# A planned attention-and-two-layers kernel: other transfer times in its planner, single score groups in the first batch, and sums of weights on GpSimd

## The chip, the cores and the metric

The kernel runs on one core of a Trainium2 chip. The metric is the device time of one execution in microseconds (us), the median of several runs. The engines are TensorE (PE in the rows; PEld is its loading of weights), VectorE (DVE), ScalarE (ACT), GpSimd (POOL) and SyncE (SP). SP and POOL issue the transfers. Each engine takes its instructions strictly in order, so an instruction that waits holds up all that are queued behind it on that engine.

## The reference

Four batches of attention with 12 heads, 448 positions and head width 64, and then two layers of a plain two-matrix network on the 1792 x 768 result:

```
scores = cap * tanh(q @ k.T / sqrt(64) / cap)          # cap = 30
attn   = exp(scores - max) / (sum(exp(scores - max)) + 1e-9)
x      = (attn @ v), heads joined                      # 1792 x 768
h      = max(x @ w_in, 0);  x = (h * h) @ w_out        # first layer, 768 -> 2048 -> 768
h2     = max(x @ w_in2, 0); out = (h2 * h2) @ w_out2   # second layer, same sizes
```

Everything is float32. The weights arrive as 64-bit words and are rounded on the chip to float32.

## The kernel before, in words

**Numbers.** TensorE multiplies in a reduced format; a float32 value is split into a high part (a rounded copy) and a low part (value minus copy), and a product takes three matmuls: high x high, high x low, low x high. In the first batch the attention weights times the values (L524, with `whole` set) are done in plain float32 instead, two matmuls in the trace for each in the code.

**First part** (until about 709 us). `unit(s)` is one row of weight tiles times one batch of the first layer: 34 units for each of four batches (`NU = 34`, `NS = 136` in all), L370 to L372. While batch b goes through its units, the attention of batch b + 1 is done in between; only batch 0 has its attention ahead of all units. A batch has six `pair`s of heads. A pair has four score groups a, b, c, d (`GROUPS`): for each, scores (L493), tanh (L498), exp (L503), then attention times values (L524). Afterwards the sums of exp are copied (`den`, L558, two ScalarE instructions), inverted (L561), multiplied in (L565) and split into `xb` (L570, L212). Scores live in the ring `sc`, which has two places; tanh and exp work in place, and in the first batch the place is free again when exp has been written to `pe`.

**Rounding weights.** `round_words` loads words (L256, L259), scales them on ScalarE (L265), puts the bits together on VectorE (L268, L271, L274) and stores the float32 weights to DRAM from the POOL queue (L277). For the first layer this runs inside batch 0's units. For the second layer it runs in 17 *blocks* (`round_block`) during batches 1 to 3: each block rounds two tiles into `wx` (ring `wg`, three buffers), and when both stores have landed, adds and subtracts their quarters in place in a chain of four sums (`one_sum`, L306) and stores the results (L310). When those stores land, the buffers of the block are free for the scaling of a later block, which stands in ScalarE's queue among the splits of weights that feed TensorE (`wh`, L332; then `wl`, L212 on VectorE; three buffers each).

**Second part** (from about 709 us). The second layer takes two batches at a time with seven products instead of eight, of weight tiles and of the sums of tiles (L821 to L823). Its first evacuated product goes to a tile `one` (L841) whose memory was that of `wx`; it waits until the last block's stores have landed.

**The order.** `Plan` collects all operations with an engine, a cost in ns, a place (about one per unit) and dependencies, and `emit` simulates them: on every engine it takes, out of a window of 40 by place, the operation that could start first by its own clock. The order that comes out is the program's; the chip's waits are then as the chip has them. A transfer is planned with 700 ns before it starts, its bytes by a rate (L105) and a fixed time until it has landed (L106). The planner knows the engine names "POOL" (issuing of transfers) and, in the change, "GP" as two queues with clocks of their own; on the chip they are one.

Of the kernel before, what the change touches and what calls it, by code (L numbers as in the profile page):

```python
# [25 lines left out]
NU = len(UNITS)  # L26
# [10 lines left out]
class Plan:  # L37
# [12 lines left out]
    def op(self, engine, cost, emit, place, deps=(), take=(), drop=(), after=()):  # L50


        self.ops.append([engine, cost, emit, place, list(deps), list(take), list(drop), None, list(after)])
        return len(self.ops) - 1

    def emit(self, sizes):
        rings = {n: [(0.0, i) for i in (range(k) if isinstance(k, int) else k)] for n, k in sizes.items()}
        for o in self.ops:
            o[5] = [r if isinstance(r, tuple) else (r, [None]) for r in o[5]]
            o[6] = [r if isinstance(r, tuple) else (r, [None]) for r in o[6]]  # L60
        for o in self.ops:
            o[4] = [d() if callable(d) else d for d in o[4]]
        waiting, clock = {}, {}
        for i in sorted(range(len(self.ops)), key=lambda i: (self.ops[i][3], i)):
            waiting.setdefault(self.ops[i][0], []).append(i)
            clock[self.ops[i][0]] = 0.0
        turn = {n: [] for n in rings}
        for i in sorted(range(len(self.ops)), key=lambda i: (self.ops[i][3], i)):
            for r, _ in self.ops[i][5]:
                turn[r].append(i)  # L70
        dma = 0.0
        while any(waiting.values()):
            best = None
            now = self.ops[waiting["PE"][0]][3] if waiting["PE"] else 1e9
            for e, ids in waiting.items():
                found = None
                for at, i in enumerate(ids[:self.WINDOW]):
                    _, _, _, place, deps, take, _, _, after = self.ops[i]
                    if place > now + self.AHEAD:
                        break  # L80
                    if any(self.ops[d][7] is None for d in deps + after):
                        continue
                    t = max([clock[e]] + [self.ops[d][7] + self.DELAY for d in deps])
                    names = [r for r, _ in take]
                    if any(len(rings[r]) < names.count(r) or turn[r][0] != i for r in names):
                        continue
                    for r in names:
                        t = max(t, sorted(rings[r])[names.count(r) - 1][0])
                    if found is None or t < found[0] - 1:
                        found = t, e, at  # L90
                    if t <= clock[e]:
                        break
                if found and (best is None or found[0] < best[0]):
                    best = found
            t, e, at = best
            op = self.ops[waiting[e].pop(at)]
            for r, cell in op[5]:
                got = min(rings[r], key=lambda x: x[0])
                rings[r].remove(got)
                cell[0] = got[1]  # L100
                turn[r].pop(0)
            op[2]()
            if e in ("SP", "POOL"):
                clock[e] = t + 60
                dma = max(dma, t + 700) + op[1] / 400  # L105
                op[7] = dma + 1300  # L106
            else:
                clock[e] = op[7] = t + op[1]
            for r, cell in op[6]:
                rings[r].append((op[7], cell[0]))  # L110
# [47 lines left out]
def pipeline(ctx: ExitStack, tc: tile.TileContext, qk, v, capt, rcap, eps, win, wout, w32, sums, x2, out):  # L158
# [13 lines left out]
    nc = tc.nc  # L172
# [27 lines left out]
    op = plan.op  # L200
# [4 lines left out]
    def dve(n, rate=1.04):  # L205
        return rate * n + 67
# [87 lines left out]
    def round_block(g, i, k, t0):  # L294


        c0, c1 = (0, HC) if g == 0 else FP[1][k]
        n = c1 - c0
        us = [unit_of(g, r, k) for r in (i, i + (HF if g == 0 else HC))]
        ms = [round_words(1, u, t0 + 2.5 * r, ring="wg") for r, u in enumerate(us)]  # L300

        def one_sum(q):
            a11, a12, a21, a22 = (m["f"][:, h * n:h * n + n] for m in ms for h in range(2))
            out, a, b, how = [(a22, a21, a22, ALU.add), (a21, a11, a21, ALU.subtract),
                              (a11, a22, a11, ALU.subtract), (a12, a12, a11, ALU.subtract)][q]
            nc.vector.tensor_tensor(out, a, b, op=how)  # L306

        def store():
            for r, m in enumerate(ms):
                nc.gpsimd.dma_start(sums[g, i][:, 2 * r:2 * r + 2, c0:c1], m["f"][:, :2 * n].rearrange("p (h c) m -> p h c m", h=2))  # L310

        o = [stored[1, u] for u in us]
        for q in range(4):
            o = [op("DVE", dve(n * 128), lambda q=q: one_sum(q), t0 + 5, o)]
        summed[g, i, k] = op("POOL", 4 * n * 128 * 512, store, t0 + 5, o, drop=[("wg", m["wf"]) for m in ms])

    def load_w(s):
        l, u = s // NS, s % NU
        nk = n_of(l, u)
        m = rings_of()  # L320

        def load():
            m["f"] = w_f[m["wf"][0]]
            nc.sync.dma_start(like(l, u, m["f"]), kept(l, u))

        split_w(s, m, [op("SP", nk * 128 * 512, load, s - 4, [stored[l, u]], take=[("wf", m["wf"])])], n=nk)
# [99 lines left out]
    def pair(b, j, t0, step, whole, on_act):  # L426
# [55 lines left out]
        for gi, tiles in enumerate(GROUPS):  # L482
            s, n = groups[gi], len(tiles) * S
# [41 lines left out]
                                         start=t == 0 and n == 0, stop=t == 3 and n == len(passes) - 1)  # L525

            t1 = t0 + dt[gi]
            if gi == 0:
                scored = []

                def both(scored=scored):
                    for x in scored:
                        x()

                first = op("PE", mm(6), both, t1, [parts], take=[("sc", x["at"]) for x in groups[:2]])
                scored.append(scores)
            elif gi == 1:
                scored.append(scores)
            if gi < 2:
                o = first  # L540
            else:
                o = op("PE", mm(3), scores, t1, [parts], take=[at], drop=["qkh", "qkl"] if gi == 3 else [])
# [46 lines left out]
    for u in range(NU):  # L589
        round_words(0, u, start + 9 + 4 * u if u < EARLY else u - 3.5, u if u < 3 or u >= EARLY else None)  # L590
        if 3 <= u < EARLY:
            load_w(u)
    for b in range(B):
        if b + 1 < B:
            for j in range(NP):
                pair(b + 1, j, b * NU + 0.5 + 4.9 * j, 1.25, (b + 1, j) in WHOLE, True)
        for u in range(NU):
            s = b * NU + u
            if b:
                load_w(s)  # L600
                if s % 6 == 4:
                    round_block(*blocks[(s - NU) // 6], s)
            unit(s)

    two = {}
# [453 lines left out]
```

## Time and profile before

| what | us |
|---|---|
| median of 3 runs | 1118.12 |
| the 3 runs | 1116.62, 1118.12, 1132.72 |
| the profiled execution, whole time | 1121.04 |
| its span, first to last instruction | 1119.3 |
| TensorE busy in the span | 1083.4 |
| VectorE busy | 840.2 |
| ScalarE busy | 725.7 |
| GpSimd busy | 74.3 |

The sum of the prediction is made against the profiled execution, 1121.04 us, which is 2.92 us above the median. A busy engine is one with an instruction of its own under way; a matmul's end is modelled, so busy TensorE isn't TensorE at its peak. Of a wait the profile names the instruction that came last.

### The profile page before, as it was taken

What the parts mean: (1) busy time and instruction counts of PE and PEld (TensorE: products, weight loads), DVE (VectorE), ACT (ScalarE), POOL (GpSimd) and SP (SyncE); (2) the same over time, 40 slices, a digit from 0 to 9 for tenths busy, and PEclk for the clock granted to TensorE, in tenths of its full rate; (3) what the DMA queues carried; (4) which work ended last, traced back from release to release, by engine and by line L of the source; (5) the groups of instructions that cost most, each with busy time, mean ns of one, the idle gap of its engine ahead of it and who ended that gap; (6) DMA issues with size and microseconds to landing.
All of it is one profiled execution on the core that took longest, in us unless ns stands there. A gap on an engine that the chain in (4) does not pass through costs nothing.

```text
span 1119.3 us, 14984 instructions
## 1 busy us (share of the span) xinstructions
PE 1083.4 (97%) x5320; PEld 939.8 (84%) x5320; DVE 840.2 (75%) x1092; ACT 725.7 (65%) x1053; POOL 74.3 (7%) x130
## 2 busy tenths in 40 slices
PE   5889999999999999999998999999999999999997
PEld 3457777888888888888887889899999999999997
DVE  4787889888889787888866885455897775569852
ACT  5798887867998777998645843344656534465641
POOL 0000011101001010001111111000000000000000
PEclk9999999999999999999999999999999999999999
DMA  8376787968666789575666886433346543333442
GB/s 223 91 235 224 233 251 226 283 201 295 191 176 227 203 274 287 164 213 172 190 220 222 305 261 205 130 107 105 99 129 208 167 142 104 113 99 121 130 133 71
DMA packets 82788, 207.92 MB, mean 186 GB/s; under 512 B 10768, under 2 KB 37264, under 8 KB 82704
## 3 DMA queue, kind: packets, MB, share of 16 engines
q1 hardware_dynamic: 72240, 163.61, 49.8%
q0 software_dynamic: 10464, 43.26, 10.1%
q8 instruction: 43, 0.70, 0.3%
q14 instruction: 41, 0.34, 0.1%
HBM read 158.07 MB, written 48.76 MB: 185 GB/s over the span
## 4 chain that ended last, share of the span: by engine, by line
PE 83%; issue 6%; DMA 4%; ACT 3%; DVE 3%; POOL 1%; SPq 0%; DVEq 0%; ACTq 0%; POOLq 0%
PE bank L821 12%; PE bank L822 12%; PE bank L823 12%; PE bank L370 11%; PE bank L372 11%; PE bank L371 10%; PE bank L524 9%; PE bank L493 5%; DMA wo<-wx 3%; ACT pe L503 1%; DVE wx L306 1%; ACT bank L498 1%; ACT d L558 1%; DMA wi<-wx 1%; POOL so L310 0%
## 5 line engine op out<-in xcount | busy, mean ns | idle before, releaser
L332 ACT ACTIVATE wh<-wf 128x768 fp32r<-128x768 f32 (+1 forms) x248 | 204.0, 824 | 230.6 <-PE bank L822 134.7
L212 DVE TENSOR_TENSOR wl<-wf,wh 128x768 fp32r<-128x768 f32 (+1 forms) x248 | 229.0, 925 | 143.2 <-ACT wh L332 139.5
L370 PE MATMUL bank<-xb,wh 128*128 128x448 f32 x384 | 146.7, 382 | 3.1 <-ACT wh L332 3.1
L370 PE MATMUL bank<-gh,wh 128*128 128x448 f32 x384 | 144.9, 377 | 0.0
L372 PE MATMUL bank<-gh,wl 128*128 128x448 f32 x384 | 141.0, 367 | 2.0 <-DVE wl L212 2.0
L372 PE MATMUL bank<-xb,wl 128*128 128x448 f32 x384 | 140.9, 367 | 1.8 <-DVE wl L212 1.8
L371 PE MATMUL bank<-gl,wh 128*128 128x448 f32 x384 | 140.9, 367 | 0.0
L371 PE MATMUL bank<-xb,wh 128*128 128x448 f32 x384 | 140.4, 366 | 0.3 <-DVE xb L212 0.3
L822 PE MATMUL bank<-xc,wh 128*128 128x448 f32 x384 | 140.2, 365 | 0.0
L821 PE MATMUL bank<-xc,wh 128*128 128x448 f32 x378 | 138.2, 366 | 1.2 <-ACT one L841 1.2
L823 PE MATMUL bank<-xc,wl 128*128 128x448 f32 x378 | 138.1, 365 | 0.0
L823 PE MATMUL bank<-xb,wl 128*128 128x448 f32 x294 | 107.4, 365 | 0.0
L821 PE MATMUL bank<-xb,wh 128*128 128x448 f32 x294 | 107.4, 365 | 0.0
L822 PE MATMUL bank<-xb,wh 128*128 128x448 f32 x288 | 105.2, 365 | 0.0
L498 ACT ACTIVATE bank<-bank,caps 128x896 f32<-128x896 f32 x96 | 83.2, 882 | 29.3 <-PE bank L493 28.3
L370 PEld LDWEIGHTS bank<-xb,wh 128*128 128x128 f32 x384 | 72.1, 188 | 18.4 <-issue 8.4
L561 DVE RECIPROCAL d<-d 128x448 f32<-128x448 f32 x24 | 70.8, 2949 | 20.6 <-ACT d L558 20.4
L370 PEld LDWEIGHTS bank<-gh,wh 128*128 128x128 f32 x384 | 72.5, 189 | 15.2 <-issue 9.2
L372 PEld LDWEIGHTS bank<-xb,wl 128*128 128x128 f32 x384 | 72.1, 188 | 9.6 <-DVE wl L212 3.9
L372 PEld LDWEIGHTS bank<-gh,wl 128*128 128x128 f32 x384 | 72.6, 189 | 8.3 <-DVE wl L212 2.4
L371 PEld LDWEIGHTS bank<-xb,wh 128*128 128x128 f32 x384 | 72.2, 188 | 8.0 <-issue 2.0
L371 PEld LDWEIGHTS bank<-gl,wh 128*128 128x128 f32 x384 | 72.6, 189 | 5.9 <-issue 0.6
(136 smaller groups left out, 1950.1 us busy)
## 6 DMA issues: line engine op xcount, KB each, us to landing
ww<-win_dram SPq DMA_DIRECT2D x27, 768.0 KB, 5.6
wf<-wi SPq DMA_DIRECT2D x48, 384.0 KB, 4.6
ww<-wout_dram SPq DMA_DIRECT2D x18, 768.0 KB, 6.3
wf<-wo SPq DMA_DIRECT2D x38, 320.0 KB, 4.1
raw<-qk_dram SPq DMA_DIRECT2D x48, 240.0 KB, 5.9
wf<-si SPq DMA_DIRECT2D x60, 192.0 KB, 2.5
wf<-wo SPq DMA_DIRECT2D x28, 384.0 KB, 3.9
wf<-wi SPq DMA_DIRECT2D x48, 192.0 KB, 2.5
```

The costliest lines, as they stand in the source:

```text
L212: nc.vector.tensor_tensor(out, a, b.bitcast(F32), op=ALU.subtract)
L332: nc.scalar.activation(m["hi"][:, :n], m["f"][:, :n], AF.Copy)
L370: nc.tensor.matmul(a, lhsT=w["hi"][:, c], rhs=x_hi, start=first and n == 0, stop=False)
L371: nc.tensor.matmul(a, lhsT=w["hi"][:, c], rhs=x_lo, start=False, stop=False)
L372: nc.tensor.matmul(a, lhsT=w["lo"][:, c], rhs=x_hi, start=False, stop=end)
L493: nc.tensor.matmul(s["s"][:, i, :S], lhsT=k[rows, S + 128 * t:S + 128 * t + 128], rhs=q[rows, :S], start=k_low + q_low == 0, stop=k_low == 1)
L498: nc.scalar.activation(s["s"], s["s"], AF.Tanh, scale=rcap)
L524: nc.tensor.matmul(pv[a][:, :S], lhsT=vt[x][rows, w:w + 128], rhs=s[y][rows, i], start=t == 0 and n == 0, stop=t == 3 and n == len(passes) ...
L561: nc.vector.reciprocal(m["d"], m["d"])
L821: nc.tensor.matmul(a, lhsT=hi, rhs=x(0), start=first and z == 0, stop=False, skip_group_check=more)
L822: nc.tensor.matmul(a, lhsT=hi, rhs=x(1), start=False, stop=False, skip_group_check=more)
L823: nc.tensor.matmul(a, lhsT=lo, rhs=x(0), start=False, stop=final and z == len(xs) - 1, skip_group_check=more)
```

## The change

Four edits. The planner takes 300 bytes per ns instead of 400 and 2500 ns instead of 1300 for a transfer (L105, L106). The four sums of a block are `nc.gpsimd` instructions, planned on a queue "GP" at a cost of 2.1 ns for each element instead of 1.04. In the first batch the scores of groups a and b are two operations, each of which takes one place of the ring `sc`; before, one operation took both places and computed both (later batches keep that). The 17 blocks are placed at units 38, 43.5, ... 126 (5.5 apart) instead of 34, 40, ... 130 (6 apart).

```diff
             if e in ("SP", "POOL"):
                 clock[e] = t + 60
-                dma = max(dma, t + 700) + op[1] / 400
-                op[7] = dma + 1300
+                dma = max(dma, t + 700) + op[1] / 300
+                op[7] = dma + 2500
...
-            nc.vector.tensor_tensor(out, a, b, op=how)
+            nc.gpsimd.tensor_tensor(out, a, b, op=how)
...
         for q in range(4):
-            o = [op("DVE", dve(n * 128), lambda q=q: one_sum(q), t0 + 5, o)]
+            o = [op("GP", dve(n * 128, 2.1), lambda q=q: one_sum(q), t0 + 5, o)]
...
-            if gi == 0:
+            if gi == 0 and b:
                 scored = []
...
-            elif gi == 1:
+            elif gi == 1 and b:
                 scored.append(scores)
-            if gi < 2:
+            if gi < 2 and b:
                 o = first
...
+    for q, block in enumerate(blocks):
+        round_block(*block, NU + 4 + 5.5 * q)
     for b in range(B):
...
             if b:
                 load_w(s)
-                if s % 6 == 4:
-                    round_block(*blocks[(s - NU) // 6], s)
             unit(s)
```

Both programs have the same number of matmuls, and the same transfers.

**TensorE, second pair of the first batch.** `qkh`, `qkl` are the pair's split queries and keys, `pe` the results of exp, `vr` the values (257 is the first pair's, 264 the second's). Before:

```order
L493 MATMUL bank_198<-qkh_288 128x448 x2
L493 MATMUL bank_198<-qkl_290,qkh_288 128x448 x2
L493 MATMUL bank_198<-qkh_288,qkl_290 128x448 x2
L493 MATMUL bank_198<-qkh_288 128x448 x2
L493 MATMUL bank_198<-qkl_290,qkh_288 128x448 x2
L493 MATMUL bank_198<-qkh_288,qkl_290 128x448 x2
L524 MATMUL bank_198<-pe_323,vr_257 128x448 x2
L493 MATMUL bank_198<-qkh_288 128x448 x2
L493 MATMUL bank_198<-qkl_290,qkh_288 128x448 x2
L493 MATMUL bank_198<-qkh_288,qkl_290 128x448 x2
L524 MATMUL bank_198<-pe_356,vr_264 128x448 x2
```

and with the change:

```order
L493 MATMUL bank_198<-qkh_289 128x448 x2
L493 MATMUL bank_198<-qkl_292,qkh_289 128x448 x2
L493 MATMUL bank_198<-qkh_289,qkl_292 128x448 x2
L524 MATMUL bank_198<-pe_310,vr_257 128x448 x2
L493 MATMUL bank_198<-qkh_289 128x448 x2
L493 MATMUL bank_198<-qkl_292,qkh_289 128x448 x2
L493 MATMUL bank_198<-qkh_289,qkl_292 128x448 x2
L524 MATMUL bank_198<-pe_322,vr_257 128x448 x2
L524 MATMUL bank_198<-pe_336,vr_264 128x448 x2
L493 MATMUL bank_198<-qkh_289 128x448 x2
L493 MATMUL bank_198<-qkl_292,qkh_289 128x448 x2
L493 MATMUL bank_198<-qkh_289,qkl_292 128x448 x2
```

Group a's scores of a pair now stand ahead of the last two value products of the pair before, and scores and value products take turns.

**GpSimd, the first block** (`wi_1_0`, `wi_1_8` are its two tiles, `si_0` its sums). Before:

```order
L277 DMA wi_1_0_130<-wx_245 128x768
L409 DMA x2_0_5_89<-y_2085 128x448
L277 DMA wi_1_8_138<-wx_245 128x768
L277 DMA wi_1_1_131<-wx_245 128x768
L310 DMA si_0_152<-wx_245 128x768 x2
```

and with the change:

```order
L277 DMA wi_1_0_130<-wx_245 128x768
L409 DMA x2_0_5_89<-y_2122 128x448
L277 DMA wi_1_8_138<-wx_245 128x768
L306 ISA
L306 TENSOR_TENSOR wx_245<-wx_245 128x384 x4
L310 DMA si_0_152<-wx_245 128x768 x2
L277 DMA wi_1_1_131<-wx_245 128x768
```

The sums stand in the queue that issues the stores, behind the two stores whose landing they wait for; the next block's first store comes behind them.

**ScalarE, the last block.** L265 scales its second tile, `one` is the first tile that takes over `wx`'s memory. Before:

```order
L265 ACTIVATE wx<-ww_244 128x512
L332 ACTIVATE wh_247<-wf_242 128x640
L332 ACTIVATE wh_248<-wf_240 128x640
L406 ACTIVATE y<-bank 128x448
L332 ACTIVATE wh_246<-wf_241 128x768
L332 ACTIVATE wh_247<-wf_242 128x640
L332 ACTIVATE wh_246<-wf_240 128x640
L332 ACTIVATE wh_248<-wf_241 128x768
```

(then one copy `y`, three more splits, and `one`), and with the change:

```order
L265 ACTIVATE wx<-ww_244 128x512
L332 ACTIVATE wh_248<-wf_240 128x640
L406 ACTIVATE y<-bank 128x448
L332 ACTIVATE wh_247<-wf_241 128x768
L332 ACTIVATE wh_246<-wf_242 128x768
L332 ACTIVATE wh_247<-wf_240 128x640
L332 ACTIVATE wh_248<-wf_241 128x768
L406 ACTIVATE y<-bank 128x448
L841 ACTIVATE one<-bank 128x448
```

Between the last scaling and `one` there are five splits of weights now; before there were nine.

## Rows read from the trace of the kernel before

**Rows 1.** The page, busy time, share of the span and instructions by engine.

```profile
PE 1083.4 (97%) x5320; PEld 939.8 (84%) x5320; DVE 840.2 (75%) x1092; ACT 725.7 (65%) x1053; POOL 74.3 (7%) x130
```

**Rows 2.** Windows: window, length, busy us (instructions) by engine, granted clock, DMA share, GB/s.

```profile
0.00:28.00 28.00, 16.45 (x63) 9.22 (x64) 12.13 (x19) 16.16 (x20) 0.88 (x5) 1.00 0.82 223
28.00:56.00 28.00, 23.62 (x97) 12.46 (x97) 21.77 (x26) 21.58 (x28) 1.08 (x2) 0.94 0.32 91
56.00:84.00 28.00, 24.14 (x110) 14.68 (x107) 24.54 (x26) 25.21 (x33) 1.08 (x2) 1.00 0.78 235
```

**Rows 3.** Waits of TensorE, whole run: total us, times, longest.

```profile
PE bank L493 <- ACT pe L503: 12.2, 9, 2.1
PE bank L493 <- DVE qkh L445: 6.5, 1, 6.5
```

**Rows 4.** Timeline, second pair: start, us, engine, line, tiles, count, idle before.

```profile
19.79 0.47 PE L493 MATMUL bank<-qkh 64*128 64x448 f32 x2
23.79 0.47 PE L493 MATMUL bank<-qkh 64*128 64x448 f32 x2 [1.75 <-ACT pe L503]
24.30 1.85 ACT L498 ACTIVATE bank<-bank,caps 128x896 f32<-128x896 f32 x2
24.59 1.77 PE L524 MATMUL bank<-pe,vr 128*128 128x448 f32 x4
26.17 1.91 ACT L503 ACTIVATE pe<-bank,caps 128x896 f32<-128x896 f32 x2
35.84 3.03 PE L524 MATMUL bank<-pe,vr 128*128 128x448 f32 x4
```

**Rows 5.** Tanh at L498 between 8 and 60 us: ScalarE's idle time before it, times.

```profile
  PE bank L493: 14.7, 8
```

**Rows 6.** Timeline of ScalarE, the copies of the last pair's sums.

```profile
78.50 1.28 ACT L558 ACTIVATE d<-bank,eps 64x448 f32<-64x448 f32 x2 [1.92 <-PE bank L524]
```

**Rows 7.** Waits of TensorE after 400 us.

```profile
PE bank L372 <- DVE wl L212: 3.8, 5, 2.0
PE bank L370 <- ACT wh L332: 3.1, 2, 2.5
PE bank L821 12%; PE bank L822 12%; PE bank L823 12%; PE bank L370 11%; PE bank L372 11%; PE bank L371 10%; PE bank L524 9%; PE bank L493 5%; DMA wo<-wx 3%; ACT pe L503 1%; DVE wx L306 1%; ACT bank L498 1%; ACT d L558 1%; DMA wi<-wx 1%; POO
```

**Rows 8.** Timeline of TensorE, its longest wait after 84 us.

```profile
600.34 0.47 PE L370 MATMUL bank<-xb,wh 128*128 128x448 f32 x1 [2.48 <-ACT wh L332]
```

**Rows 9.** Timeline of ScalarE, 560 to 660 us: scaling that waited for a store.

```profile
570.30 0.90 ACT L265 ACTIVATE wx<-ww 128x768 f32<-128x768 f32 x1 [2.83 <-DMA so<-wx]
597.46 1.67 ACT L265 ACTIVATE wx<-ww 128x768 f32<-128x768 f32 x2 [4.71 <-DMA so<-wx]
616.79 0.66 ACT L265 ACTIVATE wx<-ww 128x512 f32<-128x512 f32 x1 [4.09 <-DMA so<-wx]
```

**Rows 10.** Line L306, the sums: ns least/median/most, first and last start.

```profile
L306 DVE TENSOR_TENSOR wx<-wx x68: 416/550/560, 266.6 to 689.2; 128x384 f32<-128x384 f32 x56, 128x256 f32<-128x256 f32 x12
```

**Rows 11.** Timeline of VectorE around one block's sums.

```profile
587.31 2.34 DVE L306 TENSOR_TENSOR wx<-wx 128x384 f32<-128x384 f32 x4 [3.39 <-DMA wo<-wx]
591.27 0.96 DVE L212 TENSOR_TENSOR wl<-wf,wh 128x768 fp32r<-128x768 f32 x1 [0.21 <-ACT wh L332]
```

**Rows 12.** Timeline of ScalarE at the end of the first part.

```profile
679.72 0.66 ACT L265 ACTIVATE wx<-ww 128x512 f32<-128x512 f32 x1
691.31 0.74 ACT L332 ACTIVATE wh<-wf 128x640 fp32r<-128x640 f32 x1 [3.41 <-PE bank L371]
709.09 0.53 ACT L841 ACTIVATE one<-bank 128x448 f32<-128x448 f32 x1
```

**Rows 13.** Timeline of GpSimd, the last stores of sums.

```profile
689.88 1.44 POOL L310 DMA_DIRECT2D so<-wx  x2 [2.01 <-DVE wx L306]
```

**Rows 14.** DMA issues: count, KB each, median us from issue to landing.

```profile
so<-wx POOLq DMA_DIRECT2D x6, 256.0 KB, 4.6
```

**Rows 15.** Line L265, the scaling: ns least/median/most, first and last start.

```profile
L265 ACT ACTIVATE wx<-ww x34: 652/897/940, 244.1 to 679.7; 128x768 f32<-128x768 f32 x28, 128x512 f32<-128x512 f32 x6
```

## The prediction on record

> **What bounds the kernel now.** I read the busy times first [rows 1]: TensorE is busy for 1083.4 of 1119.3 us. The change takes no matmul away, so all that it can win is TensorE's idle time, 35.9 us, and matmuls that ran at the lower clock. Then the windows of the start [rows 2]: in the first 84 us TensorE is busy for 16.45 + 23.62 + 24.14 = 64.2 us and idle for 19.8. More than half of all idle time lies there, in the first batch's attention. The list of waits says for what [rows 3]: 6.5 us until the first queries and keys are there, which nothing here alters, and 12.2 us in nine waits for exp on ScalarE. From 400 us on TensorE waits for splits of weights, 3.8 + 3.1 = 6.9 us, and once for `one`, 1.2 us [rows 7]. The rest, 35.9 - 19.8 - 8.1 = 8.0 us, is short waits and the end of the program, which stays.
>
> **Why TensorE waits for exp at the start.** The timeline of the second pair [rows 4] shows a ring of two places used in twos. Scores of a and b start at 19.79 us, when both places are free. Group c waits until exp of a is written (23.79, after 1.75 us of idling), d for exp of b, and the next pair's a and b for both of c and d. So ScalarE runs dry as well: its tanh waited 14.7 us for scores, in eight waits, between 8 and 60 us [rows 5]. Neither engine is the bound there; they wait for each other in turn.
>
> **Why splits come late in the middle.** ScalarE's scaling for a new block stands in its queue until the stores of an earlier block's sums have landed: 2.83, 4.71 and 4.09 us [rows 9]. The splits behind it are late, and TensorE pays up to 2.48 us at once [rows 8]. On VectorE the sums themselves wait for landings, 3.39 us at 587.31, with splits of weights behind them [rows 11].
>
> **The change, part by part.**
>
> *Single score groups.* Full groups cost ScalarE 1.85 / 2 = 0.93 us of tanh and 1.91 / 2 = 0.96 of exp, 1.9 together [rows 4]. TensorE needs 0.8 us for scores (23.79 to 24.59) and 1.77 for value products alone, of which some 0.3 overlaps what follows when work is dense: 2.2 to 2.6 together. With single groups the scores of a group need only the place of the group two before; while ScalarE does tanh and exp of one, TensorE does scores of the next and values of the last. A pair then takes TensorE three of these and about 1.5 for the half group d, 8.1 to 9.3 us, and ScalarE 3 x 1.9 + 1.1 for the half group d + 1.1 for the two copies of sums (1.28 for both, less their overlap with what follows) [rows 6] + in three of the pairs 0.9 for scaling weights [rows 15] = 7.9 to 8.8. I take 8.9 for a pair, as two engines so alike never mesh quite. Now the pairs 1 to 5 take from 19.79 to 78.50 us, 58.7 / 5 = 11.7 each [rows 4, 6] (with a few of the first unit's products between). That would end the batch 5 x 2.8 = 14 us earlier. TensorE wins only what it idled or ran slowly: of 19.8 us, 6.5 stay for the inputs and about 3 in the first pair, whose first tanh has nothing before it. That leaves 10.3. To this come 1.3 us for each group of four products at the lower clock: 3.03 us at 35.84 against 1.77 at 24.59 [rows 4], with the granted clock at 0.94 over that window [rows 2]. Those are 1.2 and 2.4 GHz, and TensorE had idled before in pieces of up to 1.75 us. With the scores beside it, estimated at 0.6 more for twice their time, the stretch cost 1.9 us. Denser work should keep the clock. Against it I put 4 us of new idling, 0.4 at each pair and 1.6 at the seam, where the last pair's inversion and splits on VectorE, in series, have only the first batch-1 scores and the first half of two units to cover them. Sum: -10.3 - 1.9 + 4 = **-8 us**. Ends: -12 (nothing idles anew) and -4 (ScalarE's copies and scalings, in line with tanh, cost half of it back).
>
> *Longer transfers in the planner, blocks closer together.* This moves scalings back in ScalarE's queue to where the stores have landed. What a block needs is seen between two scalings that waited: 597.46 - 570.30 = 27.2 us and 616.79 - 597.46 = 19.3 us [rows 9]. Before, the scaling of a block's second tile came five splits after the last one in that stretch; now six to eight, at some 3.4 us each (five in the 17.0 us of the seam, below), 20 to 27 us. So most of the 6.9 us [rows 7] should go; I leave 2. **-5 us**, ends 0 and -6.9.
>
> *Sums on GpSimd.* VectorE loses 68 instructions of 0.55 us [rows 10], 37 us, and its waits for landings; it is not the bound, so this counts only through the middle term above. The cost of one sum on GpSimd is in no row. Below stands VectorE's 0.55 us for the same operation; GpSimd's own nearest row is the issue of a store, 1.44 / 2 = 0.72 us [rows 13]. I take 1.1 us, twice the nearest in kind, and twice that, 2.2, as the upper end: 4 x 0.55 = 2.2 us longer for a block, up to 6.6. The stores of `y` and of the next block queue behind the sums. A store of `y` may come 4 us late, covered by the second buffer of `y`. The Trainium skill, GPSIMD Engine Reference, section Performance versus the Vector engine, measures a two-input addition at 1.96 times VectorE's time; by it the row's 0.55 us would be an estimated 1.08, and the sum the same; no run here shows it yet.
>
> *The seam to the second part.* `one` needs the last block's stores. The last scaling started at 679.72, the last stores were issued from 689.88 and took 4.6 us after an issue of the second at 690.6, so 695.2: 15.5 us [rows 12 to 14]. `one` ran at 709.09, with 14 us to spare. Now the last scaling comes four splits later, behind the one at 691.31 [rows 12], so at 692.1 or later, and has 17.0 us. With sums of 256 instead of 384 elements, 4 x 0.4 us longer, the chain is 17.1. The cover is gone, and `one` is what is late next: **+1 us**, ends 0 and +4 (the last block begins late).
>
> *Elsewhere* the order between 84 and 560 us is dealt anew, where TensorE waits for hardly anything now: **+1 us**, ends 0 and +4.
>
> Sum: -8 - 5 + 1 + 1 = -11 us, from 1121.04 to 1110.0; the profiled execution is 2.92 us above the median, so **1107 us**. Ends: -12 - 6.9 = -18.9, which is 1099, and -4 + 0 + 4 + 4 = +4, which is 1122.
>
> **The rivals.**
>
> *The start is not where the time is.* ScalarE becomes the bound of the first batch at once: scaling, splits for the first units and copies in line, while VectorE is busy for 24.5 of 28 us from 56 on [rows 2]. For it: 25.2 of 28 us of ScalarE there. Against it: 14.7 us of ScalarE's idling is in the rows. Then only the middle gains: 1118 - 5 + 2 = 1115.
>
> *The new transfer times do not do what they say.* Blocks are planned closer together (5.5 places, not 6), so scalings wait for landings again, in other places, and with the end of the first part late by 4: 1118 - 8 + 0 + 4 = 1114.
>
> *Slower: the blocks can't keep up.* 17 blocks have from 244.1 [rows 15] to 709.09 us, 27.3 us each; this is the point that decides. The two needs above have a mean of 23.2. If every sum and a two-input VectorE operation of 0.96 us [rows 11] take turns, four sums take 4 x (1.1 + 0.96) = 8.2 us instead of 2.34, and a block 29.1. That is 1.8 us too many, 17 times: 31 us of waiting for `one`. 1118 - 8 + 31 = 1141. For it: VectorE is seldom idle where attention, rounding and splits meet, 24.54 of 28 us in the last window of [rows 2]. Against it: it needs every sum to meet one, and the mean need includes waits that the new order takes out. The Trainium skill speaks for this one, against the change: SBUF — State Buffer, section Who interferes with whom, says that a VectorE instruction with two SBUF inputs and a GpSimd instruction that reads SBUF exclude each other, the second waiting for the whole of the first. Where that holds always, the time is 1141; before, no row has both engines at it, so the trace can't say.
>
> **How the numbers follow.** Forecast 0.61, start not gained 0.14, middle not gained 0.18, blocks too slow 0.07. The likeliest gives 1107. The range goes from 1099, the sum of the best ends, to 1122, the sum of the worst, which takes in the two middle rivals; outside are the slow rival and a little of the rest. A difference of 2%, 22.4 us, is about what a measurement of this kernel can tell from no change. Faster by more would need nearly all idle time that isn't the ends': 0.03. Slower by more is most of the last rival: 0.06. Within: 0.91.
>
> **What would show it.** In the first 84 us TensorE should idle for 12 to 15 us instead of 19.8, the pairs' copies should come 8 to 10 us apart, and tanh should wait for scores for under 5 us. From 560 to 700 us the waits of scalings for landings should be under 3 us in all and TensorE's for splits under 3. A sum should take 0.8 to 1.4 us on GpSimd. `one` should wait up to 4 us. The forecast is wrong if tanh still waits 10 us or more before 60 us, if sums take over 2 us or VectorE's two-input operations grow beside them, or if TensorE stands still before `one` for over 10 us.

## The result, and the profile after

The changed kernel took **1109.37 us** (median of 9 runs, 1108.61 to 1115.40), before 1119.22 beside it (9 runs); ratio 0.9886, 95% interval 0.9843 to 0.9928. In a second set of runs (after_again, below) it was 1109.11 (6 runs, 1108.08 to 1110.19), ratio 0.9872 (0.9833 to 0.9911). Forecast were 1107, in a range from 1099 to 1122: right, if 2 us too low. But one term of the sum was wrong by some 4 us and another by 3 the other way. Three runs of the experiments below were slow, two of single_only (1185.66 and 1776.38 us, granted clocks of 0.85 and 0.56) and one of no_times (1132.61 us), and no median here contains them.

The profiled execution took 1115.40 us with a span of 1113.6, the longest of the nine; why is told first, as it concerns every comparison. The page after, busy time by engine (before: [rows 1]):

```profile
PE 1089.4 (98%) x5320; PEld 936.7 (84%) x5320; DVE 833.7 (75%) x1024; ACT 726.5 (65%) x1053; POOL 157.4 (14%) x198
```

TensorE idles for 1113.6 - 1089.4 = 24.2 us instead of 35.9, but is busy for 6 us more, with as many matmuls. The windows show where. Columns: window, length, PE busy (matmuls), granted clock, DMA share, GB/s. The second part of the changed kernel, first profile:

```profile
720.00:1000.00 280.00, 280.00 (x1357) 1.00 0.40 126
```

The same window of a second profile of the same kernel (after_again, 1109.82 us):

```profile
720.00:1000.00 280.00, 280.00 (x1384) 1.00 0.41 128
```

In 280 us without a gap, at the same granted clock, TensorE starts 1357 matmuls in one execution and 1384 in the other. The time from one start to the next, the *pitch*, is 206.67 or 202.67 ns in the mean of the second part, called 206.5 and 202.5 below. The second part lasts 417 us after its first wait, so this is some 8 us. The experiments below come back to it. What follows compares mostly waits, which it doesn't touch; busy times of two profiles can differ by it, in the first part too, if less (some 1.3 us in after_again).

*The start.* Windows of the first 84 us (PE, PEld, DVE, ACT and POOL busy, clock, DMA share, GB/s), against [rows 2]:

```profile
0.00:28.00 28.00, 19.25 (x73) 10.26 (x74) 12.13 (x19) 18.01 (x23) 0.88 (x5) 1.00 0.85 224
28.00:56.00 28.00, 26.58 (x114) 13.70 (x113) 25.16 (x29) 26.49 (x34) 1.10 (x2) 1.00 0.48 148
56.00:84.00 28.00, 26.15 (x118) 15.98 (x117) 24.82 (x29) 24.49 (x33) 1.62 (x3) 1.00 0.72 208
```

TensorE is busy for 72.0 us and idle for 12.0 instead of 19.8, and the clock stays at 1.00 where it was 0.94. From 28 to 56 us ScalarE is busy for 26.49 of 28 us, before 21.58: it and TensorE are both nearly full there. Tanh at L498 between 8 and 60 us, its idle time before it (before: [rows 5]):

```profile
  PE bank L493: 8.8, 7
```

and ScalarE's copies of the pairs' sums (before: [rows 6]), the first of the first two pairs and the last of the batch:

```profile
22.28 0.63 ACT L558 ACTIVATE d<-bank,eps 64x448 f32<-64x448 f32 x1
...
31.33 0.63 ACT L558 ACTIVATE d<-bank,eps 64x448 f32<-64x448 f32 x1
...
70.47 0.63 ACT L558 ACTIVATE d<-bank,eps 64x448 f32<-64x448 f32 x1
```

Pairs follow each other at 9.05 us, and the last copy starts at 70.47 where the last two began at 78.50.

*The middle and the seam.* TensorE's waits from 200 to 720 us (us, times, longest; before: [rows 7]):

```profile
PE bank L372 <- DVE wl L212: 3.1, 5, 1.0
PE bank L821 <- ACT one L841: 1.6, 1, 1.6
```

Scalings at L265, idle before them for stores of sums, over the whole run (before: three waits of [rows 9], 11.6 us); between 560 and 700 us, where those three lay, it is 2.8 us now:

```profile
  DMA so<-wx: 5.8, 5
```

The sums at L306 (least, median, most ns; before: [rows 10]):

```profile
L306 POOL TENSOR_TENSOR wx<-wx x68: 727/1037/2123, 260.9 to 687.4; 128x384 f32<-128x384 f32 x56, 128x256 f32<-128x256 f32 x12
```

And the last block on the timeline, its last scaling and `one` (before: [rows 12]):

```profile
677.65 0.67 ACT L265 ACTIVATE wx<-ww 128x512 f32<-128x512 f32 x1 [0.85 <-DMA so<-wx]
695.47 0.54 ACT L841 ACTIVATE one<-bank 128x448 f32<-128x448 f32 x1
```

From the scaling to `one` it takes 17.8 us, and TensorE waits 1.6 us for it.

### The profile page after: what moved, and what is told of

Read it like the earlier page. It is cut to its first block, busy times and chain, and to the rows that moved or that the text cites. A ratio compares the mean times of both kernels' runs of the same rounds, so it can differ in the third digit from the quotient of the medians.

```text
span 1113.6 us, 15010 instructions
## 1 busy us (share of the span) xinstructions
PE 1089.4 (98%) x5320; PEld 936.7 (84%) x5320; DVE 833.7 (75%) x1024; ACT 726.5 (65%) x1053; POOL 157.4 (14%) x198
## 4 chain that ended last, share of the span: by engine, by line
PE 83%; issue 7%; DVE 4%; ACT 2%; DMA 1%; POOL 1%; SPq 0%; POOLq 0%; ACTq 0%; DVEq 0%
PE bank L821 12%; PE bank L822 12%; PE bank L823 12%; PE bank L370 11%; PE bank L372 11%; PE bank L371 11%; PE bank L524 8%; PE bank L493 5%; DVE wl L212 1%; POOL wo L277 1%; DMA raw<-qk_dram 1%; DMA wo<-wf 1%; ACT pe L503 1%; ACT d L558 0%; DVE xc L212 0%
## 5 line engine op out<-in xcount | busy, mean ns | idle before, releaser
L212 DVE TENSOR_TENSOR wl<-wf,wh 128x768 fp32r<-128x768 f32 (+1 forms) x248 | 235.4, 951 | 164.5 <-ACT wh L332 163.5
L498 ACT ACTIVATE bank<-bank,caps 128x896 f32<-128x896 f32 x96 | 83.7, 885 | 25.6 <-PE bank L493 24.9
L306 POOL TENSOR_TENSOR wx<-wx 128x384 f32<-128x384 f32 (+1 forms) x68 | 80.9, 1190 | 54.7 <-DMA wi<-wx 29.7
L561 DVE RECIPROCAL d<-d 128x448 f32<-128x448 f32 x24 | 70.8, 2949 | 16.3 <-ACT d L558 16.3
L821 PEld LDWEIGHTS bank<-xc,wh 128*128 128x128 f32 x378 | 71.0, 188 | 9.1 <-ACT one L841 2.0
```

The source lines that it names most:

```text
L212: nc.vector.tensor_tensor(out, a, b.bitcast(F32), op=ALU.subtract)
L306: nc.gpsimd.tensor_tensor(out, a, b, op=how)
L498: nc.scalar.activation(s["s"], s["s"], AF.Tanh, scale=rcap)
L561: nc.vector.reciprocal(m["d"], m["d"])
L821: nc.tensor.matmul(a, lhsT=hi, rhs=x(0), start=first and z == 0, stop=False, skip_group_check=more)
```

## The experiments

Theory: single groups give some 8 us at the start; transfer times and places together give some 5 in the middle; the sums on GpSimd cost nothing of their own. Rivals: one of the two gains is not there, or GpSimd takes back a part. Each run is compared with runs of before on the same chip; where medians of before differ (1119 to 1126), its runs lie in two groups, of which more below.

**single_only**: before with single score groups in the first batch, nothing else.

```diff
-            if gi == 0:
+            if gi == 0 and b:
...
-            elif gi == 1:
+            elif gi == 1 and b:
...
-            if gi < 2:
+            if gi < 2 and b:
```

> The kernel before with the single score groups of the first batch alone. Theory (the gain is the first batch's 7 to 8 us of idling plus the middle's 5): 1110 to 1113 us; TensorE idles 12 to 13 us in the first 84 us, and the middle keeps its 6 to 7 us of waits for splits. Rival 1 (the whole gain comes from the planner's times): 1118 us, 20 us of idling at the start. Rival 2 (the gain is VectorE freed of the sums): 1118 us.

1111.83 us (10 runs, 1109.66 to 1119.35), ratio 0.9928 (0.9897 to 0.9960): 9.0 us below before's 1120.88 on the same chip by the medians, 8.1 by the ratio. Its start reads as that of the changed kernel:

```profile
28.00:56.00 28.00, 26.60 (x116) 13.77 (x113) 25.17 (x29) 26.49 (x35) 1.08 (x2) 1.00 0.48 138
```

The first term of the sum is shown, mechanism and size.

**times_only**: before with the new transfer times alone.

```diff
-                dma = max(dma, t + 700) + op[1] / 400
-                op[7] = dma + 1300
+                dma = max(dma, t + 700) + op[1] / 300
+                op[7] = dma + 2500
```

> The kernel before with the transfer times of the planner alone (300 bytes per ns, 2500 ns). Theory: 1112 to 1116 us; the scalings' waits for landings in the middle fall from 11.6 us to under 6 and TensorE's waits for splits from 6.9 to 2 or 3, the start keeps its 19 to 20 us of idling. Rival 1 (it is all the planner's times): 1107 to 1110 us. Rival 2 (VectorE freed): 1118 us.

1120.27 us, ratio 1.0007 (0.9976 to 1.0038): no gain, where 1112 to 1116 had been expected. No scaling waits for a store of sums any more, yet TensorE's waits from 200 to 720 us are these:

```profile
PE bank L821 <- ACT one L841: 7.3, 1, 7.3
PE bank L372 <- DVE wl L212: 2.6, 1, 2.6
```

and ScalarE's timeline says why:

```profile
685.25 0.65 ACT L265 ACTIVATE wx<-ww 128x512 f32<-128x512 f32 x1
705.43 0.54 ACT L841 ACTIVATE one<-bank 128x448 f32<-128x448 f32 x1 [7.18 <-DMA so<-wx]
```

The scalings were moved back to where the stores have landed; so the last one comes 5.5 us later than in [rows 12], and what was won ahead of the seam is waited for at it. That wait costs more than itself, as the clock falls behind it (last section).

**gpsimd_only**: before with the sums on GpSimd.

```diff
-            nc.vector.tensor_tensor(out, a, b, op=how)
+            nc.gpsimd.tensor_tensor(out, a, b, op=how)
...
-            o = [op("DVE", dve(n * 128), lambda q=q: one_sum(q), t0 + 5, o)]
+            o = [op("GP", dve(n * 128, 2.1), lambda q=q: one_sum(q), t0 + 5, o)]
```

> The kernel before with the sums on GpSimd alone, planned at 2.1 ns an element. Theory: 1116 to 1122 us, since the sums lie beside other work and the block chain gets some 3 us longer each while the planner still believes in early landings: ScalarE's scalings wait 10 us or more. Rival 2 (the gain is VectorE freed of the sums and their waits): 1108 to 1112 us.

1125.82 us, ratio 1.0045 (1.0015 to 1.0075): slower. TensorE waits longer for ScalarE's splits (before 3.1, 2, 2.5):

```profile
PE bank L370 <- ACT wh L332: 7.3, 2, 5.5
```

and scalings wait 15.0 us for stores of sums, before 11.6.

**no_gpsimd**: the changed kernel with the sums on VectorE (the diff above, reversed).

> The changed kernel with the sums back on VectorE, all else kept. Theory: 1107 to 1112 us, the same as the changed kernel or a little faster (blocks shorter by some 3.5 us each, no taking of turns). Rival 2 (the gain is VectorE freed): 1114 us or more, with VectorE's waits for landings of 10 us and more back and TensorE's waits for splits at 5 or more.

**1103.99 us** (1103.18 to 1104.34), ratio 0.9853 (0.9823 to 0.9883): 5 us below the changed kernel, below the 1107 to 1112 that were expected, and the fastest of all. A part of the 5 can be the chip: after_again ran on another one, and the lowest run of before beside no_gpsimd is 1115.62 us, beside the two sets of the changed kernel 1116.62 and 1116.97. By the lowest runs, less that difference, 4.4 and 3.5 us are left. Its page and its waits from 560 to 720 us:

```profile
PE 1079.5 (98%) x5320; PEld 938.1 (85%) x5320; DVE 841.1 (76%) x1092; ACT 725.7 (66%) x1053; POOL 76.1 (7%) x130
...
PE bank L821 <- ACT one L841: 1.2, 1, 1.2
```

Handing 68 sums to GpSimd, 36 us by the sum of their durations, takes VectorE from 841.1 to 833.7 us only. Most of the rest comes back as longer instructions: those that stay on VectorE add up to 865 us in no_gpsimd and to 889 in the changed kernel, 24 us more. (What is left over is overlap of instructions that follow each other closely.) VectorE's groups by shape, 250 to 690 us (busy, mean ns), before:

```profile
L212 DVE TENSOR_TENSOR wl<-wf,wh 128x768 fp32r<-128x768 f32 x64 | 60.7, 951 | 14.8 <-ACT wh L332 14.5
L212 DVE TENSOR_TENSOR pl<-bank,ph 128x896 fp32r<-128x896 f32 x36 | 39.2, 1088 | 11.0 <-ACT ph L509 10.7
L570 DVE CAST xb<-d 128x448 fp32r<-128x448 f32 x12 | 4.6, 386 | 0.0
```

and in the changed kernel:

```profile
L212 DVE TENSOR_TENSOR wl<-wf,wh 128x768 fp32r<-128x768 f32 x66 | 66.7, 1011 | 33.5 <-ACT wh L332 33.1
L212 DVE TENSOR_TENSOR pl<-bank,ph 128x896 fp32r<-128x896 f32 x33 | 35.9, 1088 | 18.1 <-ACT ph L509 17.8
L570 DVE CAST xb<-d 128x448 fp32r<-128x448 f32 x12 | 8.5, 705 | 0.0
```

Operations with one input in PSUM (`pl<-bank,ph`) keep their time to the nanosecond; the two groups above that read SBUF alone grow. Not every such form does: three inversions (L561), which read SBUF too, run beside a sum and keep their 2.95 us. What makes an operation grow is a sum at the same moment. Of the 66 splits `wl` of 128x768 in this window of the changed kernel, 12 overlap a sum in time; seven of these take 1240 to 1772 ns, five 946 to 960, and none of the other 54 over 961.

**after_again, gp_with_dve_plan, dve_with_gp_plan.** Moving the sums does two things: another engine does them, and the planner, told so, orders everything else anew. The second of these kernels lets GpSimd compute in the order planned for VectorE; the third lets VectorE compute in the order planned for GpSimd. First the changed kernel once more, unaltered.

> The changed kernel once more, unaltered. Its first profile has the matmuls of the second part 206.5 ns apart, where before, single_only, times_only and no_gpsimd have 202.5; that is 8 us of 417, and that execution was 6 us above the median of its own runs. Theory A: the stream of matmuls goes at one of two pitches, chosen anew where a wait or a matmul of another shape interrupts it, and in the second part nothing interrupts it after the wait for the last sums; then the profiled execution has 202.5 in the second part and lies at 1107 to 1111 us, or 206.5 and lies at 1114 to 1117, and the runs fall into two groups some 7 us apart, most in the lower. Theory B: sums on GpSimd slow the second part in every execution; then the pitch is 206.5 again whatever the time, and the profiled execution lies at the median, about 1109.

1109.11 us; the profiled execution took 1109.82, with 202.5 ns in the second part. B is refuted. Of theory A the two pitches hold, but not the rule that a wait or another shape draws the pitch: this same profile changes it at 640.12 us in the middle of an even stream (last section).

```diff
-            o = [op("GP", dve(n * 128, 2.1), lambda q=q: one_sum(q), t0 + 5, o)]
+            o = [op("DVE", dve(n * 128), lambda q=q: one_sum(q), t0 + 5, o)]
```

> GpSimd computes the sums, but the planner goes on taking them for VectorE's work, so TensorE, ScalarE and the rest issue in the order of no_gpsimd (1104.0 us). If what the sums on GpSimd cost is physical (a longer chain in each block, and VectorE's operations with two SBUF inputs growing beside them): 1107 to 1111 us, with waits for weights in 440 to 700 us as in the changed kernel (3.7 us idle) or more. If it is the other order that the planner makes for them: 1103 to 1105.

1110.47 us, ratio 0.9891 (0.9854 to 0.9928): six runs at 1107.7 to 1111.1 and four at 1116.0 to 1118.3. The lowest of the six lies 4.5 us above the lowest of no_gpsimd, with the same order on TensorE and ScalarE (on another chip, where the lowest run of before is 1.4 us higher, so 3 at least): the engine costs. As the order is the same, the two profiles can be laid side by side, matmul for matmul. Up to 650 us they differ by 0.6 us, all of it from the first 17 us, before any sum. Then three waits are longer with the sums on GpSimd, by 3.4 us in all: 1.29 us at 655.41, 0.97 at 666.56, and 1.1 more for `one`. The first shows how. Here is VectorE in no_gpsimd:

```profile
648.07 0.39 DVE L646 CAST xc<-four 128x448 fp32r<-128x448 f32 x1
648.37 0.55 DVE L306 TENSOR_TENSOR wx<-wx 128x384 f32<-128x384 f32 x1
648.84 0.62 DVE L212 TENSOR_TENSOR xc<-four,xc 128x448 fp32r<-128x448 f32 x1
649.37 0.56 DVE L306 TENSOR_TENSOR wx<-wx 128x384 f32<-128x384 f32 x1
649.84 0.62 DVE L212 TENSOR_TENSOR xc<-four,xc 128x448 fp32r<-128x448 f32 x1
650.38 0.62 DVE L212 TENSOR_TENSOR xb<-four,xb 128x448 fp32r<-128x448 f32 x1
650.91 1.28 DVE L627 TENSOR_TENSOR four<-four 128x448 f32<-128x448 f32 x2
652.11 0.82 DVE L212 TENSOR_TENSOR wl<-wf,wh 128x640 fp32r<-128x640 f32 x1
```

and the same work in gp_with_dve_plan, with GpSimd's row and TensorE's:

```profile
648.06 0.39 DVE L646 CAST xc<-four 128x448 fp32r<-128x448 f32 x1
648.48 2.77 DVE L212 TENSOR_TENSOR xc<-four,xc 128x448 fp32r<-128x448 f32 x2
651.17 1.43 DVE L212 TENSOR_TENSOR xb<-four,xb 128x448 fp32r<-128x448 f32 x1
652.52 2.10 DVE L627 TENSOR_TENSOR four<-four 128x448 f32<-128x448 f32 x2
654.53 0.82 DVE L212 TENSOR_TENSOR wl<-wf,wh 128x640 fp32r<-128x640 f32 x1
...
648.40 5.08 POOL L306 TENSOR_TENSOR wx<-wx 128x384 f32<-128x384 f32 x4 [6.06 <-DMA wo<-wx]
...
655.41 0.47 PE L372 MATMUL bank<-gh,wl 128*128 128x448 f32 x1 [1.29 <-DVE wl L212]
```

Both have done the cast at the same time. VectorE then does the five operations *and* two sums by 652.11, or the five operations alone by 654.53: while GpSimd has four sums under way, each of them takes up to 1.43 us instead of 0.62. The split of weights behind them comes 2.4 us later, and TensorE waits 1.29 us for it.

Now the third kernel:

```diff
-            nc.gpsimd.tensor_tensor(out, a, b, op=how)
+            nc.vector.tensor_tensor(out, a, b, op=how)
```

> The reverse: VectorE computes the sums, but everything is issued in the order that the changed kernel has for sums on GpSimd. If the engine costs, and not the order: 1103 to 1106 us, VectorE's wl and xb back at 951 and 386 to 420 ns, idle in 440 to 700 us about 1 to 2. If the order costs: 1107 to 1111 with the changed kernel's waits.

1109.44 us, ratio 0.9900 (0.9853 to 0.9947): four runs at 1107.8 to 1110.0 and two at 1116.9. So its second reading holds: with all sums back on VectorE, the order made for GpSimd costs as much by itself. TensorE's waits from 300 to 720 us:

```profile
PE bank L372 <- DVE wl L212: 1.7, 3, 0.9
PE bank L821 <- ACT one L841: 1.6, 1, 1.6
PE bank L524 <- DVE d L565: 1.0, 1, 1.0
```

So engine and order cost about as much each as both together. By the lowest runs they lie 4.5, 4.6 and 4.9 us above no_gpsimd, less 1.4 for the chip. TensorE's idle time in the profiles (span less busy time) says the same: 22.1 us in no_gpsimd, 25.4 with the engine alone, 25.3 with the order alone, 24.9 with both (after_again). The order that the planner makes for GpSimd may avoid some of the meetings and pay for it elsewhere: between 560 and 720 us TensorE idles 1.2 us in no_gpsimd, 4.5 in gp_with_dve_plan and 3.3 in after_again. This is read from the waits and not shown apart.

**no_place**: the changed kernel with the blocks at their old places.

```diff
-    for q, block in enumerate(blocks):
-        round_block(*block, NU + 4 + 5.5 * q)
...
+                if s % 6 == 4:
+                    round_block(*blocks[(s - NU) // 6], s)
```

> The changed kernel with the blocks of sums at their old places in the plan (each six units apart, the first at the second batch's fifth unit, the last later), and the new transfer times, single groups and sums on GpSimd kept. Theory: the closer places are what ends the last sums before the second part needs them; then the wait for the last sums is 5 to 9 us (times_only had 7.3 there) and the time 1113 to 1118. Rival: the places do nothing, and the time stays at 1108 to 1111 with that wait below 3.

1128.78 us, ratio 1.0046 (1.0010 to 1.0081): 19 us above the changed kernel, more than expected. Its profiled execution, 15.0 us longer than that of after_again, waits 11.7 us more for the two below; the rest is busy time, where the clock falls behind the waits (last section). The last scaling starts at 695.05, and TensorE waits for

```profile
PE bank L372 <- DVE wl L212: 8.8, 7, 2.3
PE bank L821 <- ACT one L841: 7.7, 1, 7.7
```

**place_only**: before with this one edit the other way round.

> Before with nothing but the blocks of sums at the closer places in the plan. If the places carry what the middle gained (no_place was 19 us above the changed kernel): waits in 560 to 700 us at 0 to 2 us instead of 6.9, the wait for the last sums 1 to 2.5, the time 1111 to 1115. If they act only with the new transfer times or the single groups: 1117 to 1121.

1124.61 us, ratio 1.0029 (0.9988 to 1.0071): no gain. TensorE waits 7.1 us for `wl` over the run, before 3.8 (and 0.9 for `wh`, before 3.1); scalings wait 7.7 us for stores of `so` and 5.5 for stores of `si`.

**single_and_place**: no_gpsimd with the old transfer times.

```diff
-                dma = max(dma, t + 700) + op[1] / 300
-                op[7] = dma + 2500
+                dma = max(dma, t + 700) + op[1] / 400
+                op[7] = dma + 1300
```

> no_gpsimd with the old transfer times in the planner, that is before with single groups and closer places alone. If the new transfer times bring nothing of their own: 1103 to 1106 us, as no_gpsimd (1104.0). If they bring the few us that the prediction gave them and the places together: 1107 to 1112, with the waits for wl and wh back in 560 to 700 us.

1115.97 us, ratio 0.9943 (0.9909 to 0.9977): 12 us above no_gpsimd by the medians, 10 by the ratio, and above what either reading expected. single_only has 0.9928, so on top of single groups the closer places alone bring nothing.

**no_times**: the changed kernel with the same edit.

> The changed kernel with the old transfer times. The longer blocks of GpSimd's sums could need the times that no_gpsimd does not need. If the times do nothing: 1107 to 1111 us. If they matter here: 1112 to 1118, with the scalings waiting for loads (9 to 15 us, as in the kernels with the old places) and TensorE for wl and wh.

1120.86 us, ratio 0.9994 (0.9954 to 1.0034): the whole gain is gone, more than expected. What its scalings waited for:

```profile
  DMA so<-wx: 23.0, 8
  DMA si<-wx: 9.7, 2
```

These four and times_only belong together. Either edit of the middle alone gives nothing (1.0007, 1.0029). The times without the places make the blocks end late, and TensorE waits at the seam; the places without the times put scalings ahead of the landings that they need, and TensorE waits for splits behind them. The rows show the latter in no_times (32.7 us of waiting for stores) and less clearly in place_only (13.2, before 11.6); in single_and_place scalings wait 6.9 us for stores, less than the 10.9 of single_only, so what keeps the gain away there is not shown. Together, on top of single groups, they bring 1111.83 to 1103.99. Two things stay open. The new times with single groups, without the places and GpSimd, were not run. And only one pair of times and places was: as dve_with_gp_plan shows that another order alone is worth some 3 us or more, a part of these 8 us can be luck of this one order.

**redraw_pitch**: the changed kernel with 22 more matmuls over 64 rows in the second part.

```diff
+                    if first and z == 0 and n == "A11":
+                        nc.tensor.matmul(a, lhsT=hi[:64], rhs=x(0)[:64], start=True, stop=False, skip_group_check=True)
```

> The changed kernel with 22 matmuls more in the second part, each over 64 rows, into a bank that the next matmul starts anew (the output stays as it was), one about every 19 us. Seen so far: the pitch of TensorE's stream (202.5 or 206.5 ns) changes only behind a wait or behind a matmul of another shape, and the 417 us of the second part have neither. If such an interruption draws the pitch anew: the profile of the second part has stretches of both pitches with their borders at these matmuls, and the runs do not fall into groups 7 us apart; 22 x about 0.4 us (0.2 of its own, 0.1 more at either side, as the 64-row matmuls of the first part have) is 9 us, so 1116 to 1124. If one pitch belongs to an execution as a whole or to the second part's instructions: one pitch from the first to the last of them.

1121.85 us; all 12 runs within 1120.36 to 1123.04. One of the places:

```profile
726.11 0.36 PE L825 MATMUL bank<-xb,wl 128*128 128x448 f32 x1
726.40 0.47 PE L822 MATMUL bank<-xb,wh 64*128 64x448 f32 x1
...
727.11 0.37 PE L824 MATMUL bank<-xb,wh 128*128 128x448 f32 x1
```

The three steps from 726.11 to 727.11 take 1.00 us where two take 0.405: 0.595 x 22 = 13.1 us against 12.7 measured (0.4 each had been expected). The second part has 202.5 ns between all of them, so no border was seen, and no run fell into a group 7 us higher. As the changed kernel itself had one such run in 15, this neither shows nor refutes that they draw the pitch anew. That only such interruptions do is refuted elsewhere (last section), against what the expectation gives as seen so far.

## Why the prediction was right, and where it was not

- **Where the time lay**: right. 19.8 us of idling at the start became 12.0, at the lower end of the 12 to 15 forecast, and the clock stayed up.
- **Single groups, -8**: measured -9.0 on the medians and -8.1 by the ratio (single_only). Pairs at 9.05 us against 8.9 taken. Of the signs, one missed: tanh still waits 8.8 us for scores, not under 5; yet ScalarE, with copies and scalings in the same queue, is busy for 26.49 of 28 us.
- **Times and places, -5**: the mechanism was right, the size too small: -7.8 with the sums on VectorE (single_only to no_gpsimd, on one chip). Both signs came: from 560 to 700 us TensorE's waits for splits fell under 3 (no_gpsimd: none), and those of scalings for stores to 2.8. Of the 9.0 us between the two profiled spans only 4.3 are idle time; the rest is busy time, where single_only has a clock of 0.99 from 560 to 680 us and more matmuls at the longer pitch, which the prediction didn't count. The prediction took both edits for one term and didn't say that each needs the other. The piece that it did see, that scalings moved back leave `one` without cover, is what takes the whole gain in times_only (7.3 us).
- **Sums on GpSimd, 0**: this step failed. "It is not the bound, so this counts only through the middle term" is not so: the sums cost 5 us, of which 1.0 to 1.4 can be the chip (no_gpsimd's runs end at 1104.34, the changed kernel's begin at 1108.61 and 1108.08). Their own time was right (1.1 us taken, median 1.04, mean 80.9 us / 68 = 1.19). What the sum put at nothing is that VectorE's work beside them grows, by 24 us in all, with splits behind it that TensorE waits for; the prediction had this only in the slow rival and among the signs of being wrong, and that sign came. It also put the planner's new order at 1 us, where the order alone costs 3 or more. An engine busy for 75% can be the bound in the stretches in which attention, rounding and splits meet.
- **VectorE beside a sum.** An operation of 0.62 us takes up to 1.43 beside a sum on GpSimd, and nothing grows that reads PSUM. The Trainium skill, SBUF — State Buffer, section Who interferes with whom, has VectorE with two SBUF inputs and a reading GpSimd exclude each other, and counts casts among the forms that can contend; the cast at L570, from 386 to 705 ns in the mean, agrees. The Trainium skill, GPSIMD Engine Reference, section Performance versus the Vector engine, has a ratio of 1.96 for the sum itself; the medians, 1.04 / 0.55 = 1.9, agree.
- **The slow rival**, blocks that can't keep up: not so; TensorE waits 1.6 us for `one`. It had the right place of contention, but took every sum for a meeting: most splits met none (12 of 66 met one; `wl` 951 to 1011 ns in the mean).
- **The seam, +1**: 17.1 us were worked out from the last scaling to `one`, with 17.8 measured and 0.4 more of waiting. **Elsewhere, +1**: from 84 to 560 us TensorE idles 2.9 us in after_again (84 to 300) and 0.2 (300 to 560), before 1.7 and 0.1: +1.3.
- **The sum**: -9.0 - 7.8 + 5 = -11.8, measured -9.9 on the medians, -12.8 by the ratio, forecast -11. What the first two terms gave beyond the forecast, 3.8 us, and the 2 set aside for seam and elsewhere offset the 5 that GpSimd took. That the total came out so near is luck.

## What to carry to other kernels

An operation given to GpSimd can be paid for by VectorE's operations on SBUF that run beside it: compare VectorE's busy time before and after (here 36 us given, 7 gained), not the instructions moved. A planner's delays and the places of its work are one setting: too short delays put waits into a queue ahead of others' work, longer ones move the end, so change both together and look at the next seam. Before two profiles are compared, count the matmuls in an undisturbed window of each. And where a planner sets the order, run the new order with the old engine: else the two can't be told apart.

## What the runs showed of the hardware

**TensorE's stream has two pitches at the same granted clock.** Of the 14 executions profiled, five have 206.5 ns between the 448-column matmuls of the second part (the first of the changed kernel, gpsimd_only, gp_with_dve_plan, single_and_place, no_times), nine 202.5, before among these. The longer pitch comes with VectorE's sums as well as with GpSimd's, as single_and_place shows:

```profile
720.00:1000.00 280.00, 280.00 (x1356) 1.00 0.41 127
```

In the first part too the pitch changes, in before for instance to 206.5 ns from 591 to 597.5 us, behind a step of 0.32 us at 590.57. But it needs no interruption: in after_again 351 matmuls of one shape follow each other without a wait from 574.6 to 646.8 us, and the pitch changes at 640.12. Ten steps take 2.07 us up to there and 2.02 behind it:

```profile
638.05 0.37 PE L370 MATMUL bank<-gh,wh 128*128 128x448 f32 x1
...
640.12 0.37 PE L371 MATMUL bank<-gl,wh 128*128 128x448 f32 x1
...
642.14 0.37 PE L372 MATMUL bank<-gh,wl 128*128 128x448 f32 x1
```

single_only changes the other way at 616 us, again in an even stream. In the second part of all 14 profiles the pitch stays what it was at the start: 417 us x 4 / 202.5 = 8 us. All five executions at 206.5 lie in the upper part of their kernel's runs: 1115.4 against 1108.6 to 1111.6; 1116.0 with three others, against six at 1111.1 and below; 1132.5, the highest of gpsimd_only; 1123.1 in single_and_place, 0.4 below its highest; 1128.0 against a least of 1114.9. The runs of before have two such groups (1116 to 1122 and 1124 to 1132); that these are the two pitches is likely but not shown, as no profile of before fell into the upper one. What sets the pitch stays open.

**Behind the longest waits the clock fell.** In no_place TensorE waits 7.7 us for `one`, until 710.72. Behind it the granted clock is at the lower of its two levels, 1.2 instead of 2.4 GHz:

```profile
711.00:716.00 5.00, 5.00 (x14) 4.45 (x15) 1.91 (x3) 1.27 (x2) 0.00 (x0) 0.50 0.00 0
```

Matmuls start 0.37 us apart or more there, and from 680 to 720 us TensorE starts 146 of them, against 190 in after_again. times_only has the same 0.50 from 706 to 710 us, behind its 7.3 us. In no_gpsimd and after_again, where the longest wait after 84 us is 1.2 and 1.6 us, the clock stays at 1.00 from there to 1000 us.

**An edit to one engine acts through the planner as well.** The lowest run of dve_with_gp_plan lies 4.6 us above the lowest of no_gpsimd, some 3 when the difference of the chips is taken off: the order alone costs that, with not one instruction on another engine.
